# The first block of x loaded as two halves of 64 rows, one on each hardware DMA queue

## The chip, the cores and the metric

The kernel runs on one core of one Trainium2 chip. The metric is the device time of one execution in microseconds (us). The timed runs of the kernel before gave 225.97, 226.27 and 227.02 us, median 226.27.

## The reference

Two branches work on the same normalised x and are added to x: a local, dilated attention (A) and a gated mixer over the sequence (B). x is 2048 rows of 512, everything in bf16.

```python
x = A_x                                   # [1, 2048, 512]
xn = _layernorm(x, axis=-1)
return x + _A_ref(xn, A_wqkv, A_wo) + _B_ref(xn, B_w_in, B_w_sp, B_b_sp, B_w_out)

# A: 32 heads of 16; each position attends to 8 positions, 2 apart, up to itself
qkv = (xn @ wqkv) ...
logits = einsum('bhsd,bhswd->bhsw', q, kg) * scale ; softmax over the 8 ; times v ; @ wo

# B: w_in [512, 1792], w_sp [2048, 2048], w_out [896, 512]
z = _gelu(xn @ w_in)
z1 = z[..., :896] ; z2 = _layernorm(z[..., 896:])
g = einsum('ts,bsf->btf', w_sp, z2) + b_sp
return einsum('bsf,fd->bsd', z1 * g, w_out)
```

## The kernel before

The program is a list of tasks. Each task has an engine, what it reads and writes, and a name; a planner turns the reads and writes into semaphore waits. The order of the tasks on each engine is written out by hand in `plan.orders`: one list for TensorE (PE), ScalarE (ACT), VectorE (DVE), GpSimd (POOL) and the queue of SyncE (SP), in this order. Loads from HBM are issued by SP and by ACT, each into its own hardware queue. An engine takes its list strictly in order; a DMA stands in the list of the engine that issues it.

x is cut into 16 blocks of 128 rows. For each block b the planner has these tasks, all in `ln_block`: `bnst` (mean and variance statistics on DVE, L665), `bnag` (their aggregation on DVE, L668), `rstd` (the inverse root on POOL, L670), `norm` (subtract and multiply on DVE, L680). Blocks 0 to 3 are then transposed on PE (`xTr`, L696) and moved from PSUM to SBUF by ACT (`xTe`, L703); the others are transposed by DMA (`xTd`, L684).

Block 0 is treated apart, so that the first products can start before `rstd0` is there. Its rows are only centred: `ctr1` on DVE (columns 256 to 511, L673) and `ctr0` on ACT (columns 0 to 255, L675), transposed as `xTr0b` and `xTr0a`, and multiplied with w_in; `rstd0` comes in as a scale when the products are evacuated (`z2g`, L913). The products of blocks 0 to 3 with the second half of w_in are `z2_b_h` with a last letter a or b (L906): h is the half of the columns, b the half of the contraction that holds `w_in2a_1` or `w_in2b_1`, a the other. Block 0 uses half b first. The normalised block 0 for the attention is transposed later (`xNr`, L717).

The first loads are `ldx0` and `ldx1` on SP (L603), `ldw_in2a` and `ldw_in2b` in two halves each, half 0 on SP and half 1 on ACT (L608), `ldx2` on ACT, `ldx3` on SP. The next one on SP, `ldx4`, waits for `ldw_in2b_1`, and behind it stand `ldx5`, `ldx6` and `ldk` (the weights of K, L620). `ldk` and later `ldq` feed the products of Q and K (L749).

Before block 0 is there, PE runs `warm`: 29 matmuls of 146 columns on constants (L637). `fill0` (one of 256 columns) and `fill1` (three of 146) stand between the first transposes. On ACT the list begins with `actprime` (L643), which brings in the table for gelu.

The lists that matter at the start, in the kernel before:

```python
# PE
warm xTr0b fill0 xTr0a fill1 z2_0_0b z2_0_1b z2_0_0a xTr1a xTr1b z2_0_1a xNr z2_1_0a ...
# ACT
actprime ldw_in2a_1 ldw_in2b_1 ldx2 ctr0 xTe0b xTe0a xTe1a xTe1b xNe z2g0_0 ...
# DVE
zeros steps0 steps1 bnst0 bnag0 ctr1 bnst1 bnag1 norm0 norm1 bnst2 bnag2 bnst3 norm2 ...
# SP
ldx0 ldx1 ldw_in2a_0 ldw_in2b_0 ldx3 ldx4 ldx5 ldx6 ldk ldx7 ...
```

Of the kernel before, what the change touches and what calls it, by code (L numbers as in the profile page):

```python
# [328 lines left out]
def build_kernel(nc, A_x, A_wqkv, A_wo, B_x, B_w_in, B_w_sp, B_b_sp, B_w_out, out, report=False, sched_kw=None,  # L329
# [14 lines left out]
    x2 = A_x[0]  # L344
# [75 lines left out]
    with ExitStack() as es:  # L420
# [10 lines left out]
        def A(name, n, o2_=0):  # L431
            return ar[:, off[name] + o2_: off[name] + o2_ + n]

        def AC(o_, dims):
            return bass.AP(tensor=ar, offset=o_, ap=[[AR, 128]] + [list(d) for d in dims])

        def Fv(name, n, o2_=0):
            return fp[:, foff[name] + o2_: foff[name] + o2_ + n]
# [105 lines left out]
        def c_mm(n):  # L544
            return max(25.0, n / 2.4 + 2.6)

        def c_act(n, psum=True, accum=False):
            return 171.0 + n * 0.832 + (20.0 if accum else 0.0)
# [6 lines left out]
        def dma(eng, fn, nbytes, chan, reads=(), writes=(), name="", xbar=False, prio=None, lat=1700.0):  # L555
            return T(eng, fn, reads=tuple(reads), writes=tuple(writes), name=name, prio=prio,
                     dma=dict(chan=chan, nbytes=nbytes, xbar=xbar, lat=lat))
# [10 lines left out]
          name="steps0")  # L568
        T("dve", lambda v: v.memset(FCa(foff["st6"] + 8, [[9, NB], [1, 1]]), LN_EPS * D), writes=["st_eps"], est=160,
          name="steps1")  # L570
# [5 lines left out]
          writes=["ident"], est=350, name="ident1")  # L576
# [3 lines left out]
          writes=["nident"], est=350, name="nident1")  # L580
        T("pool", lambda g: g.memset(AC(off["KT"], [[KW, 4], [1, KP]]), 0.0),
          writes=[("KTpad", c, 0) for c in range(4)], est=200, name="ktpad", prio=2)
# [15 lines left out]
        def xin_ap(sl):  # L598
            return A("xin", 512, 512 * sl) if sl < 4 else A("xin2", 512, 512 * (sl - 4))

        def ld_x(b, eng="sp", after=()):
            sl = b % 8
            dma(eng, lambda e: e.dma_start(xin_ap(sl), x2[128 * b:128 * b + 128, :]), 128 * 512 * 2,  # L603
                ("xin", sl), reads=after, writes=[("xin", sl)], name="ldx%d" % b)
# [5 lines left out]
                    B_w_in[256 * h: 256 * h + 256, FH + lo: FH + lo + n].rearrange("(c p) n -> p c n", p=128)))(h),  # L610
                    256 * n * 2, (nm, h), writes=[(nm, h)], name="ld%s_%d" % (nm, h))

        ld_x(0)
        ld_x(1)
        ld_win_h("w_in2a", 0, HF)
        ld_win_h("w_in2b", HF, HF)
# [2 lines left out]
        for which, eng in ((0, "sp"), (1, "sp")):  # L619
# [4 lines left out]
                writes=[(("wq", "wk")[which], c) for c in range(4)],  # L624
                name="ld%s" % ("qk"[which]))
# [7 lines left out]
        def filler(n, name, est, prio=None, reads=(), w=512):  # L633
            def warm(t):
                last = None
                for i in range(n):
                    last = t.matmul(ps[:, 3584: 3584 + w], ones[:, :128], ones[:, :w], start=True, stop=True)  # L637
                return last
            T("pe", warm, reads=reads, writes=[("ps", 7)], est=est, name=name, prio=prio)
# [4 lines left out]
          est=-1200, name="actprime", tbl="gelu")  # L644
# [4 lines left out]
        def next_bank():  # L649
            k = ring[0]  # L650
            ring[0] = (k + 1) % NR[0]
            return k
# [8 lines left out]
        def ln_block(b):  # L661
            sl = b % 4
            xs_ = b % 8
            xin = xin_ap(xs_)
            T("dve", lambda v: v.bn_stats(Fv("st6", 6, 9 * b), xin),  # L665
              reads=[("xin", xs_)], writes=[("st6", b)],
              est=690, name="bnst%d" % b)
            T("dve", lambda v: v.bn_aggr(Fv("mv", 2, 2 * b), Fv("st6", 9, 9 * b)), reads=[("st6", b), "st_eps"],  # L668
              writes=[("mv", b)], est=180, name="bnag%d" % b)
            T("pool", lambda g: g.tensor_tensor(Fv("rstd", 1, b), Fv("mv", 1, 2 * b + 1), Fv("mhalf", 1), ALU.pow),  # L670
              reads=[("mv", b), "mhalf"], writes=[("rstd", b)], est=580, name="rstd%d" % b)
            if b == 0:
                T("dve", lambda v: v.tensor_scalar(A("attn", 256, 256), xin[:, 256: 512], Fv("mv", 1, 2 * b), None, ALU.subtract),  # L673
                  reads=[("xin", xs_), ("mv", b)], writes=[("xc", 1)], est=250, name="ctr1")
                T("act", lambda a: a.activation(A("attn", 256), xin[:, 0: 256], ACTF.Identity, bias=Fv("mv", 1, 2 * b),  # L675
                                                scale=-1.0),
                  reads=[("xin", xs_), ("mv", b)], writes=[("xc", 0)], est=400, name="ctr0")
            xo = off["attn"] + 1024 if b == 0 else off["xn"] + 512 * sl
            xk = "xn0" if b == 0 else ("xn", sl)
            T("dve", lambda v: v.tensor_scalar(AC(xo, [[1, 512]]), xin, Fv("mv", 1, 2 * b),  # L680
                                               Fv("rstd", 1, b), ALU.subtract, ALU.mult),
              reads=[("xin", xs_), ("mv", b), ("rstd", b)], writes=[xk], est=400, name="norm%d" % b)
            if b >= XDMA:
                dma("sp", lambda e: e.dma_start_transpose(AC(off["xnT"] + 128 * b, [[S, 4], [1, 128]]),  # L684
                                                          AC(xo, [[1, 512]])),
                    128 * 512 * 2, ("xT", sl), reads=[xk], writes=[("xnT", b)], name="xTd%d" % b, xbar=True)
            if b >= XDMA:
                return
            src, sk = (off["attn"], lambda h: ("xc", h)) if b == 0 else (xo, lambda h: xk)
            for h in ((1, 0) if b == 0 else (0, 1)):  # L690
                k = next_bank()

                def tr(t, h=h, k=k):
                    last = None
                    for i in range(2):
                        last = t.matmul(ps[:, 512 * k + 128 * i: 512 * k + 128 * i + 128],  # L696
                                        AC(src + 256 * h + 128 * i, [[1, 128]]), nident if b == 0 and h == 0 else ident,
                                        start=True, stop=True)
                    return last
                T("pe", tr, reads=[sk(h), "nident" if b == 0 and h == 0 else "ident"], writes=[("ps", k)], est=2 * c_mm(128), name="xTr%d%s" % (b, "ab"[h]))  # L700
                dst = (AC(off["attn"] + 512 + 256 * h, [[128, 2], [1, 128]]) if b == 0 else
                       AC(off["xnT"] + 2 * h * S + 128 * b, [[S, 2], [1, 128]]))
                T("act", (lambda dst, k: lambda a: a.activation(  # L703
                    dst, ps[:, 512 * k: 512 * k + 256].rearrange("p (c n) -> p c n", c=2), ACTF.Copy))(dst, k),
                  reads=[("ps", k)], writes=[("xcT", h) if b == 0 else ("xnTh", b, h)], est=c_act(256) - 30,
                  name="xTe%d%s" % (b, "ab"[h]))
            if b == 0:
                filler(cfg["fill0"], "fill0", 160.0 * cfg["fill0"], reads=[("xc", 1)], w=256)
                filler(cfg["fill1"], "fill1", 120.0 * cfg["fill1"], reads=[("xc", 0)], w=146)
# [389 lines left out]
        for j in range(NJ):  # L1099
# [8 lines left out]
            if j == 0:  # L1108
                for fn_, b, k0 in ((ln_block, 0, 3), (ln_block, 1, 1), (z2_block, 0, 5), (xn0_T, 0, 3), (ln_block, 2, 3), (z2_block, 1, 7),
                                   (z2_block, 2, 1), (ln_block, 3, 3), (z2_block, 3, 3)):  # L1110
                    ring[0] = k0
                    fn_(b)
                setup_masks()
                ring[0] = 5
            else:
                for b in bl:
                    ln_block(b)
            if j == 1:
# [5 lines left out]
                  name="biasf")  # L1124
# [146 lines left out]
        for t in range(NT):  # L1271
# [11 lines left out]
            if t >= 1:  # L1283
# [15 lines left out]
                out7_0 out5_0 P6_7 out4_0 P7_7 P3_7 P2_7 P4_7 out2_0 out3_0 out0_0 out1_1 out1_0 out1_2  # L1299
            """.split(),  # L1300
            """
                actprime ldw_in2a_1 ldw_in2b_1 ldx2 ctr0 xTe0b xTe0a xTe1a xTe1b xNe z2g0_0 xTe2a xTe2b z2g0_1 z2g1_0
                xTe3a xTe3b z2g2_0 z2g1_1 z2g3_0 z2g3_1 z2g2_1 QKe0_0 z2s0 QKe0_1 QKe0_2 QKe0_3 z2s1 QKe1_0 z2s2
                QKe1_1 halo0_2 QKe1_2 QKe1_3 z2s3 z2g4 halo0_1 z2g5 halo0_3 halo0_0 z2s4 halo1_1 halo1_0 z2g6 halo1_2
                z2g7 z2s5 QKe2_0 z2s6 QKe2_1 QKe2_2 z2s7 QKe2_3 z2g8 z2s8 z2g9 z2g10 z2s9 z2g11 z2s10 QKe3_0 z2s11
# [29 lines left out]
                rstd6 rstd7 rstd10 rstd8 rstd11 rstd9 rstd13 rstd14 rstd12 rstd15 hm2 zr0 zr1 zr2 zr3 srec1 srec0  # L1335
            """.split(),
            """
                ldx0 ldx1 ldw_in2a_0 ldw_in2b_0 ldx3 ldx4 ldx5 ldx6 ldk ldx7 ldx10 ldx8 ldq ldx11 xTd4 xTd5 xTd6 xTd7
                ldx9 ldx14 ldx13 ldx12 xTd10 xTd11 ldx15 xTd8 xTd9 ldwv xTd14 ldb xTd12 xTd13 xTd15 ldw_in1 w0_1 w0_0
                ldwout pT3 pT2 pT1 Vhalo0a Vzero w1_0 w1_1 ldwo1 ldwo2 ldwo3 ldwo0 Vhalo0b w2_0 w2_1 Vhalo1b Vhalo2b  # L1340
                pT0 uT15 uT14 OTd0 w3_0 w3_1 w4_0 uT12 w4_1 OTd1 uT13 Vhalo1a uT10 w5_0 OTd2 uT11 w5_1 uT8 uT9 w6_0
# [22 lines left out]
def bass_parallel_sum__sliding_local_dilated__mixer_gmlp__prompt_kernel(  # L1364
    nc, A_x, A_wqkv, A_wo, B_x, B_w_in, B_w_sp, B_b_sp, B_w_out, out
):
    build_kernel(nc, A_x, A_wqkv, A_wo, B_x, B_w_in, B_w_sp, B_b_sp, B_w_out, out)
# [28 lines left out]
```

## Time and profile before

| what | value |
|---|---|
| median of three timed runs | 226.27 us (225.97 to 227.02) |
| the profiled execution | 225.37 us, of which the span is 223.6 us |
| PE / DVE / ACT / POOL busy | 98% / 93% / 60% / 40% of the span |
| first warm-up matmul | 0.84 us |
| first transpose of block 0 | 4.41 us |
| first product with w_in | 5.22 us |
| DMA, from 0 to 5.22 us | 213 GB/s in the mean |

Times in the profile count from the start of the span. A row of the timeline gives start, length, engine, line, operation, output and input, the shapes, and how many instructions are merged in it; in brackets stands how long the engine was idle before, and what ended that. "PEld" is TensorE's loading of weights, which can run beside its matmuls. SPq and ACTq are the issues of DMAs by SP and ACT; their length is the issue alone, and the list of DMA issues tells how long after it the data had landed. Matmuls overlap in the records and their ends are modelled, so the distance from start to start is what one costs.

### The profile page before, as it was taken

Reading aid. Unit: us, or ns where it says so; the run is one execution under the profiler, and the core shown is the slowest. Engines: PE = TensorE matmul, PEld = TensorE weight load, DVE = VectorE, ACT = ScalarE, POOL = GpSimd, SP = SyncE. Lnnn points to the kernel's source line nnn. Section 1 sums busy time; section 2 is a strip of 40 time slices with the busy share of each in tenths; the row PEclk is TensorE's granted clock in tenths of the full one; section 3 lists DMA queues with packets and bytes.
Section 4 is the critical chain, followed back from the end, with each engine's and each line's share of the span. In section 5 each row is a group of like instructions: output and inputs, shape, how many; then the busy total and the mean of one; then the engine's idle time right before and its main releaser. Section 6 shows DMA issues by size and latency. Waiting matters only on the chain.

```text
span 223.6 us, 3124 instructions
## 1 busy us (share of the span) xinstructions
PE 219.7 (98%) x1166; PEld 122.4 (55%) x1180; DVE 207.3 (93%) x236; ACT 134.2 (60%) x241; POOL 89.6 (40%) x38
## 2 busy tenths in 40 slices
PE   8999999999999999999999999999999999999995
PEld 7555555554677776655555454544545544444544
DVE  4699999999999999999999999999999999999810
ACT  4769899999999999977333304324304216224442
POOL 4355559965000090000000899945999900000000
DMA  6884442790000002879689997949589696428352
GB/s 222 275 185 117 97 117 51 197 201 0 3 0 0 0 0 85 176 199 215 154 166 174 233 130 157 186 118 200 173 165 228 140 193 154 99 51 179 118 104 94
DMA packets 77716, 29.96 MB, mean 134 GB/s; under 512 B 68731, under 2 KB 75401, under 8 KB 77702
## 3 DMA queue, kind: packets, MB, share of 16 engines
q1 hardware_dynamic: 74566, 25.08, 53.2%
q10 hardware_dynamic: 3136, 4.69, 6.4%
q8 instruction: 9, 0.15, 0.3%
q14 instruction: 5, 0.04, 0.1%
HBM read 9.05 MB, written 2.10 MB: 50 GB/s over the span
## 4 chain that ended last, share of the span: by engine, by line
PE 98%; issue 0%; ACT 0%
PE ps L1044 38%; PE ps L749 12%; PE ps L926 11%; PE ps L1255 11%; PE ps L883 8%; PE ps L733 6%; PE ps L1251 6%; PE ps L906 3%; PE ps L637 2%; PE ps L807 1%; PE ps L696 0%; ACT arena L703 0%; ACT arena L1264 0%; PE ps L717 0%; PE ps L1237 0%
## 5 line engine op out<-in xcount | busy, mean ns | idle before, releaser
L1044 PE MATMUL ps<-arena 128*128 128x448 f16 (+1 forms) x448 | 86.7, 352 | 0.0
L866 POOL TENSOR_TENSOR arena<-arena,fpool 128x128 bf16<-128x128 f32 x2 | 49.9, 24946 | 45.6 <-DVE arena L862 45.6
L1044 PEld LDWEIGHTS ps<-arena 128*128 128x128 f16 (+1 forms) x448 | 43.8, 98 | 41.4
L1189 DVE TENSOR_TENSOR arena<-arena 128x4096 bf16<-128x4096 bf16 x16 | 36.2, 2282 | 0.0
L772 DVE TENSOR_TENSOR arena<-arena 128x8192 bf16<-128x8192 bf16 (+1 forms) x10 | 35.5, 3555 | 0.0
L955 POOL TENSOR_TENSOR fpool<-fpool 128x4 f32<-128x4 f32 x4 | 18.1, 4541 | 27.3 <-DVE fpool L952 27.3
L749 PE MATMUL ps<-arena 128*128 128x512 bf16 x124 | 27.7, 379 | 0.2
L1193 DVE TENSOR_TENSOR arena<-arena 128x4096 bf16<-128x4096 bf16 (+1 forms) x16 | 27.9, 1745 | 0.0
L1059 ACT ACTIVATE ps<-ps 128x448 f32<-128x448 f32 x16 | 8.4, 527 | 32.4 <-PE ps L1044 24.7
L1255 PE MATMUL ps<-arena 128*128 128x512 bf16 (+2 forms) x125 | 27.1, 355 | 0.1
L780 DVE TENSOR_TENSOR arena<-arena 128x4096 bf16<-128x4096 bf16 (+1 forms) x9 | 26.9, 2992 | 0.1
L926 PE MATMUL ps<-arena 128*128 128x448 bf16 x128 | 24.7, 352 | 0.0
L670 POOL TENSOR_TENSOR fpool<-fpool 128x1 f32<-128x1 f32 x16 | 17.4, 1088 | 16.0 <-DVE fpool L668 15.7
L1062 ACT ACTIVATE arena<-ps,fpool 128x448 bf16<-128x448 f32 x16 | 10.0, 635 | 22.3 <-PE ps L1044 22.3
L926 PEld LDWEIGHTS ps<-arena 128*128 128x128 bf16 x128 | 18.5, 144 | 5.9
L749 PEld LDWEIGHTS ps<-arena 128*128 128x128 bf16 x128 | 14.5, 113 | 13.0
L1264 ACT ACTIVATE arena<-ps 128x512 bf16<-128x512 f32 (+2 forms) x17 | 9.5, 563 | 16.8 <-PE ps L1255 16.8
L883 PE MATMUL ps<-arena 128*128 128x448 bf16 x96 | 19.1, 353 | 0.0
L1255 PEld LDWEIGHTS ps<-arena 128*128 128x128 bf16 x126 | 11.9, 98 | 12.4
L757 ACT ACTIVATE arena<-ps 128x1024 bf16<-128x1024 f32 x16 | 16.1, 1028 | 2.9 <-PE ps L749 2.8
L1251 PE MATMUL ps<-arena 128*128 128x512 bf16 (+2 forms) x65 | 15.3, 353 | 0.4
L938 ACT ACTIVATE arena<-arena 128x896 bf16<-128x896 bf16 x16 | 15.3, 956 | 0.0
(86 smaller groups left out, 256.1 us busy)
## 6 DMA issues: line engine op xcount, KB each, us to landing
arena<-in_A_x_dram ACTq DMA_DIRECT2D x8, 256.0 KB, 3.6
arena<-in_A_x_dram SPq DMA_DIRECT2D x15, 128.0 KB, 3.1
out_dram<-arena ACTq DMA_DIRECT2D x7, 256.0 KB, 2.3
arena<-in_A_wqkv_dram SPq DMA_DIRECT2D x3, 512.0 KB, 4.9
arena<-in_B_w_in_dram SPq DMA_DIRECT2D x1, 896.0 KB, 5.4
arena<-in_B_w_out_dram SPq DMA_DIRECT2D x1, 896.0 KB, 6.5
arena<-arena SPq DMA_DIRECT2D x2, 448.0 KB, 4.4
arena<-arena SPq DMA_DIRECT2D x1, 672.0 KB, 5.4
```

Of the source, the lines that this page charges most:

```text
L749: last = t.matmul(bank(k + which), AC(off["wqk"] + 1024 * dc + col0, [[4, 128]]), AC(off["xnT"] + dc * S + 512 * j, [[1, 512]]), start=(dc ...
L772: T("dve", lambda v: v.tensor_tensor(pbv, qb, kb, ALU.mult), reads=[(t_, c, j) for t_ in ("QT", "KT", "KTpad") for c in cs], writes=[("pb" ...
L780: T("dve", lambda v: v.tensor_tensor(av, av, bv, ALU.add), reads=[("pb", s_) for s_ in b], writes=[("pb", s_) for s_ in a], est=c_dve(4096 ...
L866: T("pool", lambda g: g.tensor_tensor(Rv, Zv, FCa(foff["mone"], [[0, 128]]), ALU.pow), reads=[kz, "mone"], writes=[kr], est=20000, name="s ...
L883: last = t.matmul(ps[:, 512 * (k + hf): 512 * (k + hf) + HF], AC(off["xnT"] + dc * S + 128 * b, [[1, 128]]), AC(off["w_in2"] + FH * dc + H ...
L926: lastm = t.matmul(ps[:, 512 * (k + hf): 512 * (k + hf) + HF], AC(off["xnT"] + dc * S + b, [[NTOK, 128]]), AC(off["w_in1"] + FH * dc + HF ...
L955: T("pool", lambda g: g.tensor_tensor(Fv("rstd2", 4, 4 * j), Fv("msq", 4, 4 * j), mhalf, ALU.pow), reads=[("msq", j), "mhalf"], writes=[(" ...
L1044: last = t_.matmul(pb_(k_), st(k), mv(k), start=(start and k == 0), stop=(k == 7), skip_group_check=True)
L1189: T("dve", (lambda iv, tv, av: lambda v: v.tensor_tensor(tv, iv, av, ALU.mult))(iv, tv, av), reads=[("attn", q // 4)] + [("V", i_) for i_ ...
L1193: T("dve", (lambda n: lambda v: v.tensor_tensor(AC(off["Vs"], [[4096, 2], [1, n]]), AC(off["Vs"], [[4096, 2], [1, n]]), AC(off["Vs"] + n, ...
L1251: t_.matmul(po, AC(off["OT"] + 1024 * (t % 3) + 512 * r_ + 128 * cc, [[1, 128]]), AC(off["wo"] + 512 * cc + c0, [[1, n]]), start=False, st ...
L1255: last = t_.matmul(po, AC(off["z1"] + FH * tb + 128 * fc, [[1, 128]]), AC(off["w_out"] + 512 * fc + c0, [[1, n]]), start=False, stop=(fc = ...
```

## The change

`ldx0` becomes `ldx0a` (rows 0 to 63, issued by SP, first in its list as `ldx0` was) and `ldx0b` (rows 64 to 127, issued by ACT, behind `actprime` and ahead of `ldw_in2a_1`). Each half has a semaphore of its own. `bnst0`, `ctr1`, `ctr0` and `norm0` are declared to read both halves; since `ctr1`, `ctr0` and `norm0` follow the statistics of block 0, only `bnst0` gets a wait for a second semaphore. The lists of PE, DVE and POOL stay as they are, and so does the count of warm-up matmuls; on DVE, `norm1` still stands ahead of `bnst2`.

```diff
-        ld_x(0)
+        for h in range(2):
+            dma(("sp", "act")[h], (lambda h: lambda e: e.dma_start(xin_ap(0)[64 * h: 64 * h + 64, :], x2[64 * h: 64 * h + 64, :]))(h),
+                64 * 512 * 2, (("xin", 0), "xin0b")[h], writes=[(("xin", 0), "xin0b")[h]], name="ldx0%s" % "ab"[h])
         ld_x(1)
...
             T("dve", lambda v: v.bn_stats(Fv("st6", 6, 9 * b), xin),
-              reads=[("xin", xs_)], writes=[("st6", b)],
+              reads=[("xin", xs_)] + (["xin0b"] if b == 0 else []), writes=[("st6", b)],
...
             if b == 0:
                 T("dve", lambda v: v.tensor_scalar(A("attn", 256, 256), xin[:, 256: 512], Fv("mv", 1, 2 * b), None, ALU.subtract),
-                  reads=[("xin", xs_), ("mv", b)], writes=[("xc", 1)], est=250, name="ctr1")
+                  reads=[("xin", xs_), "xin0b", ("mv", b)], writes=[("xc", 1)], est=250, name="ctr1")
                 T("act", lambda a: a.activation(A("attn", 256), xin[:, 0: 256], ACTF.Identity, bias=Fv("mv", 1, 2 * b),
                                                 scale=-1.0),
-                  reads=[("xin", xs_), ("mv", b)], writes=[("xc", 0)], est=400, name="ctr0")
+                  reads=[("xin", xs_), "xin0b", ("mv", b)], writes=[("xc", 0)], est=400, name="ctr0")
...
-              reads=[("xin", xs_), ("mv", b), ("rstd", b)], writes=[xk], est=400, name="norm%d" % b)
+              reads=[("xin", xs_), ("mv", b), ("rstd", b)] + (["xin0b"] if b == 0 else []), writes=[xk], est=400, name="norm%d" % b)
...
-                actprime ldw_in2a_1 ldw_in2b_1 ldx2 ctr0 xTe0b xTe0a xTe1a xTe1b xNe z2g0_0 xTe2a xTe2b z2g0_1 z2g1_0
+                actprime ldx0b ldw_in2a_1 ldw_in2b_1 ldx2 ctr0 xTe0b xTe0a xTe1a xTe1b xNe z2g0_0 xTe2a xTe2b z2g0_1 z2g1_0
...
-                ldx0 ldx1 ldw_in2a_0 ldw_in2b_0 ldx3 ldx4 ldx5 ldx6 ldk ldx7 ldx10 ldx8 ldq ldx11 xTd4 xTd5 xTd6 xTd7
+                ldx0a ldx1 ldw_in2a_0 ldw_in2b_0 ldx3 ldx4 ldx5 ldx6 ldk ldx7 ldx10 ldx8 ldq ldx11 xTd4 xTd5 xTd6 xTd7
```

## The prediction

> **What bounds the kernel now.** I read the page first: the busy time of each engine and the chain of work that ended last.
>
> ```profile
> span 223.6 us, 3124 instructions
> ...
> PE 219.7 (98%) x1166; PEld 122.4 (55%) x1180; DVE 207.3 (93%) x236; ACT 134.2 (60%) x241; POOL 89.6 (40%) x38
> ...
> PE 98%; issue 0%; ACT 0%
> ```
>
> TensorE (PE) is busy for 98% of the span, and the chain followed back from the last instruction is PE for 98% of it. So almost the whole kernel is one row of matmuls, and a change at the start counts by how far it moves the first useful matmul; behind that, PE has nothing to catch up with. Next I read the same chain in order of time at its beginning:
>
> ```profile
> 0.84 3.69 PE ps L637 x29
> 4.53 0.23 PE ps L696 x2
> ...
> 4.78 0.40 ACT arena L703
> ...
> 5.22 1.31 PE ps L906 x6
> ```
>
> The columns are start, length, what. L637 is the warm-up, 29 matmuls on constants; L696 the transposes of block 0 of x; L703 their evacuation by ScalarE (ACT); L906 the first products with w_in. The chain puts the warm-up ahead of the transposes, not the load of x. Ends of matmuls are modelled, so I looked at starts, in the timeline of PE alone and with its weight loads (PEld):
>
> ```profile
> 3.96 0.57 PE L637 MATMUL ps<-const-bfloat16-1.0 128*128 128x146 bf16 x3
> ...
> 4.08 0.45 PE L637 MATMUL ps<-const-bfloat16-1.0 128*128 128x146 bf16 x2
> ...
> 4.38 0.14 PEld L696 LDWEIGHTS ps<-arena 128*128 128x128 bf16 x2 [0.15 <-issue]
> 4.41 0.33 PE L696 MATMUL ps<-arena 128*128 128x128 bf16 x2
> 4.58 0.27 PE L637 MATMUL ps<-const-bfloat16-1.0 128*128 128x256 bf16 x1
> 4.69 0.28 PE L696 MATMUL ps<-arena 128*128 128x128 bf16 x2
> ```
>
> The last three warm-up matmuls start at 3.96, 4.08 and (the same step of 0.12 on) 4.20; the next slot is 4.32. The first transpose starts at 4.41. So PE stands idle for 0.09 us between the two, and its weight load (which takes the centred x) stood idle for 0.15. This 0.09 is all that an earlier x can win at this place, because PE takes its instructions in order and the 29 warm-up matmuls stay.
>
> What the transpose waits for is seen on VectorE (DVE):
>
> ```profile
> 3.02 0.69 DVE L665 BATCH_NORM_STATS2 fpool<-arena 128x6 f32<-128x512 bf16 x1 [1.61 <-DMA arena<-in_A_x_dram]
> 3.75 0.20 DVE L668 BATCH_NORM_AGGREGATE fpool<-fpool 128x2 f32<-128x9 f32 x1
> 3.98 0.29 DVE L673 TENSOR_SCALAR arena<-arena,fpool 128x256 bf16<-128x256 bf16 x1
> 4.18 0.69 DVE L665 BATCH_NORM_STATS2 fpool<-arena 128x6 f32<-128x512 bf16 x1
> ```
>
> bnst0 waits 1.61 us for x, then bnag0 and ctr1 follow with no gap to speak of; ctr1 ends at 3.98 + 0.29 = 4.27, and the weight load follows at 4.38. The two chains, warm-up and x, therefore meet within 0.09 us. A delay of x passes to PE in full; a gain is cut off at 0.09.
>
> **The change, part by part.** First the issues and their landings, from the timeline of the queues and from the list of DMA issues in narrow stretches (the last number is us from issue to landing, to one decimal):
>
> ```profile
> 0.80 0.40 SPq L603 DMA_DIRECT2D arena<-in_A_x_dram  x1
> 1.26 0.42 SPq L603 DMA_DIRECT2D arena<-in_A_x_dram  x1
> 1.72 0.95 SPq L608 DMA_DIRECT2D arena<-in_B_w_in_dram  x2
> 0.94 0.95 ACTq L608 DMA_DIRECT2D arena<-in_B_w_in_dram  x2
> 1.93 0.49 ACTq L603 DMA_DIRECT2D arena<-in_A_x_dram  x1
> 4.73 0.34 SPq L603 DMA_DIRECT2D arena<-in_A_x_dram  x1
> 6.06 0.44 SPq L620 DMA_DIRECT2D arena<-in_A_wqkv_dram  x1
> ```
>
> ```profile
> arena<-in_A_x_dram SPq DMA_DIRECT2D x1, 128.0 KB, 2.2
> arena<-in_A_x_dram SPq DMA_DIRECT2D x1, 128.0 KB, 2.8
> arena<-in_B_w_in_dram ACTq DMA_DIRECT2D x1, 224.0 KB, 2.8
> arena<-in_B_w_in_dram ACTq DMA_DIRECT2D x1, 224.0 KB, 3.3
> arena<-in_B_w_in_dram SPq DMA_DIRECT2D x1, 224.0 KB, 4.3
> arena<-in_A_x_dram ACTq DMA_DIRECT2D x1, 128.0 KB, 3.7
> arena<-in_A_wqkv_dram SPq DMA_DIRECT2D x1, 512.0 KB, 4.9
> ...
> arena<-in_B_b_sp_dram SPq DMA_DIRECT2D x1, 4.0 KB, 1.8
> ```
>
> In that order these are ldx0 (lands at 0.80 + 2.2 = 3.0), ldx1 (1.26 + 2.8 = 4.06), ldw_in2a_1 (0.94 + 2.8 = 3.74), ldw_in2b_1 (about 1.41 + 3.3 = 4.7), ldw_in2b_0 (about 2.19 + 4.3 = 6.5), ldx2 (1.93 + 3.7 = 5.63), ldk (6.06 + 4.9 = 10.96), and the smallest load of the kernel.
>
> *Block 0 in two halves.* SP still issues at 0.80, but 64 rows; ACT issues the other 64 rows at 0.94, where ldw_in2a_1 went out. bnst0 now needs both. No row shows a load of 64 rows, so I bound its landing. Early end: no faster than the 4 KB load, 1.8 us, which gives 0.94 + 1.8 = 2.74, that is 0.26 before 3.0. Late end: as slow as the first DMA of the ACT queue is now, with 3.5 times the bytes, 2.8 us: 0.94 + 2.8 = 3.74, 0.74 late. Between them stands the whole block's own 2.2: 0.94 + 2.2 = 3.14, 0.14 late. What speaks for the early side is the bandwidth, from the busy time by stretches (last two columns: DMA share and GB/s):
>
> ```profile
> 2.00:3.00 1.00, 1.00 (x11) 1.00 (x10) 0.00 (x0) 0.29 (x2) 0.25 (x2) 1.00 0.85 245
> 3.00:4.00 1.00, 1.00 (x11) 1.00 (x10) 0.91 (x3) 0.02 (x1) 0.00 (x0) 1.00 1.08 373
> ```
>
> From 2.00 to 3.00 the core moved 245 KB, nearly twice the 131 KB of block 0; the rest went to ldx1 and to ldw_in2a_1, which shared the engines with it. With both queues carrying x first, half of the traffic ahead of its landing goes away. I therefore take a landing about 0.1 us earlier than now, 2.9, nearest to the block's own row. Then ctr1 ends at 4.17, the weight load could stand at 4.28, and PE is free at 4.32: the transposes start at 4.32 and not at 4.41. Between 0 and 0.09, I count **0.05** us, since the weight load has itself to come ahead of the slot.
>
> The Trainium skill, DMA: Bandwidth & Descriptors, section Rules for kernel authors, says of two transfers to disjoint partition halves that they serialize, as both spread over the same 16 engines, and advises one transfer of 128 partitions. By that rule the split wins nothing, and the second half's landing goes with its issue, which is rival 1 below. No row of this trace shows a split load, so the trace neither agrees nor disagrees.
>
> *The second wait of bnst0.* Behind bnst0 on DVE stand bnag0, ctr1, bnst1 and all that follows, but they need block 0 anyway. DVE was idle for 1.61 us there, so a wait already fulfilled is hidden by that; uncovered it would cost about the gap between bnst0 and bnag0, 3.75 - 3.71 = 0.04. I count 0.
>
> *What ACT's queue moves.* One more issue of 0.40 to 0.49 us pushes ldw_in2a_1, ldw_in2b_1 and ldx2 back by about 0.45. ACT's own next work, ctr0, waits for DVE until 3.98, while the issues end at 1.93 + 0.49 + 0.45 = 2.87: covered. The data is wanted by these:
>
> ```profile
> 5.61 0.73 PE L906 MATMUL ps<-arena 128*128 128x448 bf16 x3
> 6.17 0.68 DVE L665 BATCH_NORM_STATS2 fpool<-arena 128x6 f32<-128x512 bf16 x1
> 6.31 0.27 PEld L696 LDWEIGHTS ps<-arena 128*128 128x128 bf16 x4 [0.22 <-DVE arena L680]
> 6.58 0.11 PEld L906 LDWEIGHTS ps<-arena 128*128 128x128 bf16 x2
> 12.15 3.75 PEld L749 LDWEIGHTS ps<-arena 128*128 128x128 bf16 x18
> ```
>
> ldw_in2a_1: 3.74 + 0.45 = 4.19 against the first product at 5.22, 1.0 us of cover. ldw_in2b_1: 4.7 + 0.45 = 5.15 against its first use, the third product at 5.61, 0.46 of cover. ldx2: 5.63 + 0.45 = 6.08 against bnst2 at 6.17, 0.09 of cover, and what stands behind bnst2 is the transpose of block 2, not the next matmul. Counted at 0; without their cover each costs PE what it is late. The SP queue's next issue behind ldx3 waits for ldw_in2b_1: ldx4 at 4.73 becomes about 5.18, and with it ldx5, ldx6 and ldk. ldk then lands at 10.96 + 0.45 = 11.41 against 12.15, when its weights are first loaded: 0.74 of cover.
>
> *What SP's queue moves.* ldx0a may be issued a little shorter (0.40 down to the 0.34 of the row at 4.73), so ldx1 and ldw_in2a_0 and ldw_in2b_0 go out 0 to 0.06 earlier, with fewer bytes of ACT's queue beside them. ldw_in2b_0 lands at 6.5 for a weight load at 6.58 that the transposes of block 1 precede; this is the tightest landing, and it gets looser. The transposes of block 1 load at 6.31 behind norm1; norm1's chain starts with bnst1 at 4.18, just behind ldx1's landing at 4.06, and moves with it. Counted at 0.
>
> *Sum.* 225.37 us for the profiled execution (its span of 223.6 and 1.77 around it) - 0.05 = 225.32. The profiled execution lies 0.90 under the median of the three timed runs, 226.27, so on that scale the forecast is 226.27 - 0.05 = 226.22, and the same 0.90 is added to each rival.
>
> **The rivals.**
>
> 1. *The second half comes later than the whole block did.* At 3.14 bnst0 is 0.14 late, ctr1 ends at 4.41, and PE waits: + 0.14, 226.4. At the far end, 3.74, it is + 0.74, 227.0. For it: the ACT queue issues 0.14 behind SP, and its first DMA took 2.8. Against it: that DMA had 224 KB.
>
> 2. *Slower by the clock.* The warm-up ran 146 columns in 0.12 us, 1.2 a ns; the 256-column filler at 4.58 was followed at 4.69, 2.3 a ns. So the array doubled its pace at about 4.5, though the granted clock reads 1.00 in both stretches above. If x is over 0.1 late, PE idles from 4.32 across this moment; if the doubling then fails and needs another stretch like the warm-up's 3.69 us at half pace, half of that is lost: + 1.85, 228.1. For it: the two moments lie within 0.2 us. Against it: 3.5 us of unbroken matmuls precede either way. The Trainium skill, TensorE: Matmul & The Clock Gate, Part 1, says that the clock is released after a busy window of about 3.4 us whose start does not depend on the kernel. The pace in these rows agrees with its two speeds; whether the window can be missed, no run here shows.
>
> 3. *The pushed-back weights arrive too late.* If ldw_in2b_1 needs the 4.3 us that the slowest load of its size took, it lands at 1.86 + 4.3 = 6.16, 0.55 behind its use: + 0.55, 226.8; the products behind it wait with it. Against it: DMA moves the same bytes in total.
>
> 4. *The gain is larger than the gap.* If the whole 0.26 of the early bound reached PE (were the warm-up not in the way): - 0.26, 226.0. Against it: the steps of 0.12 up to 4.20.
>
> **How the numbers follow.** Forecast 0.45; rival 1 0.23; rival 2 0.07; rival 3 0.12; rival 4 0.13. The predicted time is the forecast's, 226.2. The timed runs reach from 225.97 to 227.02, 1.05 wide, and the profiled execution was at 225.37, so a median of other runs can lie some tenths off by itself. The range goes from 225.3 (rival 4 less 0.7 of scatter) to 227.4 (the far end of rival 1 and 0.4 of scatter); it leaves rival 2 and the ends of scatter out, under 2 in 10. Half a per cent, 1.13 us, is about what a measurement of this kernel can tell from no change. Only rival 2 passes it by itself. To its 0.07 I add 0.08 for the far ends of rivals 1 and 3 with scatter on top: slower 0.15. No row carries a gain of 1.13; scatter on the forecast and on rival 4 gets 0.09. The rest, 0.76, is the same.
>
> **What would show it.** In the changed profile bnst0 should start between 2.76 and 3.0, the last warm-up matmul still near 4.20, the first transpose at 4.32 to 4.41, the first product at 5.13 to 5.22, and the products behind it in steps without new gaps. ACT should show three issues from 0.94 and ldx2 near 2.4; ldx4 about 0.45 later. A bnst0 after 3.1 with a transpose after 4.5 shows rival 1; products of 448 columns in steps of 0.37 after 5.2 rival 2; a gap before the third product rival 3. A span over 1 us away from 223.6 with the first product still near 5.2 would show that I looked at the wrong place.

## The result, and the profile after

| | kernel before | changed kernel |
|---|---|---|
| median of 22 runs each, taken side by side | 225.74 us (225.29 to 227.02) | 226.85 us (226.33 to 228.78) |
| ratio | | 1.0057, 95% interval 1.0040 to 1.0074 |
| profiled execution, its span | 225.37 us, 223.6 | 227.04 us, 225.3 |

The changed kernel is slower, by 1.11 us of the medians, which is 0.49%. The ratio, 1.0057, is that of the means; three runs of the changed kernel above 228.5 us pull it up. One lies just under and the other just over the half per cent, 1.13 us, that the prediction took as the bound of no change; the interval excludes a ratio of 1. The two profiled executions stand 1.67 apart, and the first thing to settle is which number is to be explained. The profiled execution of before was 0.37 under the median of these runs. A second profile of the kernel before, at 225.75 us and so at the median, is the better one to compare with; the profile of the changed kernel stands 1.29 above it. Its timeline of VectorE (DVE) and TensorE (PE):

```profile
3.44 0.69 DVE L665 BATCH_NORM_STATS2 fpool<-arena 128x6 f32<-128x512 bf16 x1 [2.03 <-DMA arena<-in_A_x_dram]
...
5.58 1.31 PE L906 MATMUL ps<-arena 128*128 128x448 bf16 x6
...
8.71 0.39 PE L696 MATMUL ps<-arena 128*128 128x128 bf16 x4
```

Here block 0 landed 0.4 us later than in the profile of the prediction, and the products with w_in started at 5.58 instead of 5.22; all six then ran through, the third at 5.58 + 2 x 0.19 = 5.96. The row at 8.71 is the transposes of block 2. Now the changed kernel. Its page, and the beginning of its chain in order of time (start, length, what):

```profile
span 225.3 us, 3126 instructions
...
PE 96%; DMA 2%; ACT 0%; issue 0%; ACTq 0%
```

```profile
0.80 0.68 ACT L645
...
1.52 0.78 ACTq L608
...
2.34 4.70 DMA arena<-in_B_w_in_dram
...
7.08 0.93 PE ps L908 x4
```

A load of w_in has entered the chain: 4.70 us of it, issued by ACT at 2.34, and PE goes on at 7.08. (The only load in the chain of the second profile of before is block 0 of x, 2.61 us.) The line numbers are two higher than before. The timeline of PE, its weight loads (PEld) and DVE shows the place:

```profile
3.35 0.69 DVE L667 BATCH_NORM_STATS2 fpool<-arena 128x6 f32<-128x512 bf16 x1 [1.95 <-DMA arena<-in_A_x_dram]
...
4.66 0.40 PE L698 MATMUL ps<-arena 128*128 128x128 bf16 x2
4.85 0.42 PE L639 MATMUL ps<-const-bfloat16-1.0 128*128 128x256 bf16 x1
5.06 0.42 PE L698 MATMUL ps<-arena 128*128 128x128 bf16 x2
...
5.85 0.76 PE L908 MATMUL ps<-arena 128*128 128x448 bf16 x2
7.08 0.93 PE L908 MATMUL ps<-arena 128*128 128x448 bf16 x4 [0.47 <-DMA arena<-in_B_w_in_dram]
...
7.91 0.70 DVE L667 BATCH_NORM_STATS2 fpool<-arena 128x6 f32<-128x512 bf16 x1 [1.32 <-DMA arena<-in_A_x_dram]
...
9.96 0.23 PEld L698 LDWEIGHTS ps<-arena 128*128 128x128 bf16 x4 [0.43 <-DVE arena L682]
9.97 0.40 PE L698 MATMUL ps<-arena 128*128 128x128 bf16 x4
```

PE runs the two products that need `ldw_in2a_1`, and then stands until `ldw_in2b_1` is there. The third product starts at 7.08, 1.12 us behind 5.96. `bnst2` too waits 1.32 us, for `ldx2`, and with it the transposes of block 2 come a little later still: 9.97 against 8.71, which is 1.26 of the 1.29 between the two executions. Block 0 itself was not the trouble: `bnst0` at 3.35 is no later than the 3.44 of before at its median.

One more thing in these rows could be taken for the cause. PE was at half pace from the transposes through the first two products: the filler of 256 columns at 4.85 is followed at 5.06, 0.21 later, where it was 0.11 in the rows of the prediction, and the two products take 0.76 us. By itself this would have held the third product until 5.85 + 0.76 = 6.61. It does not decide. In two other executions below, the second one of the changed kernel and the one with an unread load, the first two products ran at full pace (0.54 and 0.55 us), and the third still started only at 7.38 and 6.90.

The issues on both queues, and then the landings (last number, us from issue) of `ldw_in2a_1`, `ldw_in2b_1`, `ldw_in2b_0` and `ldx2`:

```profile
0.80 0.59 SPq L614 DMA_DIRECT2D arena<-in_A_x_dram  x1
1.45 0.56 SPq L603 DMA_DIRECT2D arena<-in_A_x_dram  x1
2.05 0.95 SPq L608 DMA_DIRECT2D arena<-in_B_w_in_dram  x2
...
0.94 0.55 ACTq L614 DMA_DIRECT2D arena<-in_A_x_dram  x1
1.52 0.79 ACTq L608 DMA_DIRECT2D arena<-in_B_w_in_dram  x1
2.34 0.49 ACTq L608 DMA_DIRECT2D arena<-in_B_w_in_dram  x1
```

```profile
arena<-in_B_w_in_dram ACTq DMA_DIRECT2D x1, 224.0 KB, 4.2
...
arena<-in_B_w_in_dram ACTq DMA_DIRECT2D x1, 224.0 KB, 4.7
...
arena<-in_B_w_in_dram SPq DMA_DIRECT2D x1, 224.0 KB, 5.0
arena<-in_A_x_dram ACTq DMA_DIRECT2D x1, 128.0 KB, 5.0
```

Two things went wrong at once. The issues became longer: a load of 64 rows takes 0.55 to 0.59 us to issue where the whole block took 0.40, and the load behind it takes 0.56 on SP and 0.79 on ACT. So `ldw_in2b_1` goes out at 2.34 and not at 1.41. And it takes 4.7 us instead of 3.3. It lands at 7.04, 2.3 us later than in the profile of the prediction and 2.0 later than in the second one of before (1.41 + 3.6 = 5.0).

### The profile page after: what moved, and what is told of

The parts are those of the page before. It is cut to its first block, busy times and chain, and to the rows that moved or that the text cites. A ratio compares the mean times of both kernels' runs of the same rounds, so it can differ in the third digit from the quotient of the medians.

```text
span 225.3 us, 3126 instructions
## 1 busy us (share of the span) xinstructions
PE 220.8 (98%) x1166; PEld 122.5 (54%) x1180; DVE 207.4 (92%) x236; ACT 134.3 (60%) x241; POOL 89.5 (40%) x38
## 4 chain that ended last, share of the span: by engine, by line
PE 96%; DMA 2%; ACT 0%; issue 0%; ACTq 0%
PE ps L1046 38%; PE ps L751 12%; PE ps L928 11%; PE ps L1257 11%; PE ps L885 8%; PE ps L735 6%; PE ps L1253 6%; PE ps L908 3%; DMA arena<-in_B_w_in_dram 2%; PE ps L809 1%; PE ps L698 0%; ACTq L608 0%; ACT L645 0%; ACT arena L1266 0%; PE ps L719 0%
```

## The experiments

The theories: (1) the weights of ACT's queue are late, because a load was put ahead of them and because of the order in which two queues are served; (2) the halves of 64 rows are slow in themselves; (3) the first packets of w_in are slow, which shows only when x no longer runs beside them. All ratios are to the kernel before on the same chip.

**An extra load of 64 rows on ACT, block 0 whole.** The load goes to a place that is read only much later, after it is written anew.

```diff
         ld_x(0)
+        dma("act", lambda e: e.dma_start(A("Za", 512)[64: 128, :], x2[64: 128, :]), 64 * 512 * 2, "spare", writes=["Za"], name="ldspare")
...
-                actprime ldw_in2a_1 ldw_in2b_1 ldx2 ctr0
+                actprime ldspare ldw_in2a_1 ldw_in2b_1 ldx2 ctr0
```

> Block 0 is loaded whole by SP as in the kernel before; ACT first issues a load of 64 rows of x into a place nobody reads until much later, then its weights. Theory 1, starved weights (what hurts is a small issue ahead of the weights on ACT's queue): bnst0 starts at 3.0 to 3.1 as before, but ldw_in2b_1 is issued over 0.5 us later than its 1.41 and lands near 7.0, PE waits for it, and the time is 0.8 to 1.3 us over the kernel before. Theory 2, slow halves (what hurts is that block 0 itself lands 0.33 us later, and with it the start of PE at half clock): bnst0 at 3.0, first product at 5.2, time within 0.3 us of before.

227.0 us, 1.0063 (1.0040 to 1.0087): as slow as the changed kernel. In its timeline:

```profile
3.17 0.69 DVE L666 BATCH_NORM_STATS2 fpool<-arena 128x6 f32<-128x512 bf16 x1 [1.76 <-DMA arena<-in_A_x_dram]
...
5.88 0.55 PE L907 MATMUL ps<-arena 128*128 128x448 bf16 x2 [0.63 <-DMA arena<-in_B_w_in_dram]
6.90 0.93 PE L907 MATMUL ps<-arena 128*128 128x448 bf16 x4 [0.47 <-DMA arena<-in_B_w_in_dram]
```

Block 0 is on time and the third product is at 6.90, in an execution 0.34 under its median. The loss needs no split of block 0; a small load ahead of ACT's weights is enough.

**Both halves on SP.**

```diff
-            dma(("sp", "act")[h], ...
+            dma("sp", ...
...
-                actprime ldx0b ldw_in2a_1 ...
+                actprime ldw_in2a_1 ...
...
-                ldx0a ldx1 ldw_in2a_0 ...
+                ldx0a ldx0b ldx1 ldw_in2a_0 ...
```

> Both halves of block 0 are issued by SP, one behind the other; ACT's list is that of the kernel before. Theory 1: ldw_in2b_1 is issued near 1.4 and lands near 4.7 again; SP's own weights go out one issue later, so ldw_in2b_0 lands 0.4 to 0.5 us later than 6.5 and PE waits at most that: 0.3 to 0.6 us over before. Theory 2: the two loads of 64 rows take 0.55 to 0.6 us each to issue as in the changed kernel, bnst0 starts after 3.4, and the time is at least as bad as the changed kernel's, 1.1 us or more over before.

227.44 us, 1.0071 (1.0047 to 1.0094). ACT's weights go out early again, from 0.94, but now block 0 and block 1 are late:

```profile
0.94 1.22 ACTq L608 DMA_DIRECT2D arena<-in_B_w_in_dram  x2
...
4.42 0.69 DVE L667 BATCH_NORM_STATS2 fpool<-arena 128x6 f32<-128x512 bf16 x1 [3.02 <-DMA arena<-in_A_x_dram]
...
8.58 0.40 PE L698 MATMUL ps<-arena 128*128 128x128 bf16 x4 [0.79 <-DVE arena L682]
```

The time is what theory 2 expected, but its cause is mixed: SP's two issues took 1.22 us together, and `ldx1` behind them landed at 6.45. It doesn't tell the theories apart. It does show that a long issue reaches over to the other queue: ACT's list holds no load of 64 rows here, and its two weights took 1.22 us to issue where 0.95 was usual, `ldx2` 0.62 where it was 0.49.

**The changed kernel with the two halves of ACT's weights as one load.**

```diff
+            if nm == "w_in2a":
+                dma("act", lambda e: e.dma_start(
+                    AC(off["w_in2"] + 2 * FH, [[FH, 2], [1, FH]]),
+                    B_w_in[256: 512, FH: 2 * FH].rearrange("(c p) n -> p c n", p=128)),
+                    256 * FH * 2, (nm, 1), writes=[("w_in2a", 1), ("w_in2b", 1)], name="ldw_in2_1")
-            for h in range(2):
+            for h in range(1):
...
-                actprime ldx0b ldw_in2a_1 ldw_in2b_1 ldx2 ctr0
+                actprime ldx0b ldw_in2_1 ldx2 ctr0
```

> The changed kernel, but ldw_in2a_1 and ldw_in2b_1 are one DMA of 448 KB, so ACT issues three loads ahead of its work, as many as the kernel before. Theory 1: the bytes are queued one issue earlier, the weights land by 5.6, PE's wait for them goes, and the time is within 0.4 us of before. Theory 2: bnst0 still starts near 3.35 and the time stays 0.8 to 1.3 us over before.

227.4 us, 1.0071 (1.0046 to 1.0096), spread from 226.46 to 229.05. One issue fewer doesn't cure it: the load goes out at 1.52, takes 0.79 to issue and lands at 6.4 (in an execution 0.67 under the median). Theory 1 was too simple where it counted issues only.

**Halves of 256 columns instead of 64 rows.** The same bytes on the same queues, but each half has all 128 rows.

```diff
-xin_ap(0)[64 * h: 64 * h + 64, :], x2[64 * h: 64 * h + 64, :]
+xin_ap(0)[:, 256 * h: 256 * h + 256], x2[0: 128, 256 * h: 256 * h + 256]
```

> The changed kernel, but the halves are 256 columns of all 128 rows each, not 64 rows of all columns. Theory 1: as the changed kernel, ldw_in2b_1 near 7.0 and 0.8 to 1.3 us over before. Theory 2, if it is the 64 rows that make the issue slow: issues of 0.40 to 0.43 us, first bytes near 1.7 us, and the time within 0.4 us of before.

226.3 us, 1.0022 (1.0010 to 1.0034): about half of the loss is gone, which is between what the two theories expected.

```profile
0.80 0.40 SPq L614 DMA_DIRECT2D arena<-in_A_x_dram  x1
...
0.94 0.39 ACTq L614 DMA_DIRECT2D arena<-in_A_x_dram  x1
1.36 0.97 ACTq L608 DMA_DIRECT2D arena<-in_B_w_in_dram  x2
...
2.92 0.69 DVE L667 BATCH_NORM_STATS2 fpool<-arena 128x6 f32<-128x512 bf16 x1 [1.51 <-DMA arena<-in_A_x_dram]
...
6.89 0.93 PE L908 MATMUL ps<-arena 128*128 128x448 bf16 x4 [0.63 <-DMA arena<-in_B_w_in_dram]
```

Issues are back at 0.39 and 0.40, the loads behind them at their usual length, and `bnst0` starts at 2.92. So the long issue belongs to the 64 rows and not to the 64 KB. What is left, 0.5 us, goes with the load ahead of the weights: PE still waits for `ldw_in2b_1`, until 6.89 in this execution, which was 0.4 over its median.

**Halves of columns and one load for ACT's weights.** Both edits above together.

> Block 0 in two halves of columns, one on each queue, and ldw_in2a_1 and ldw_in2b_1 as one load of 448 KB. Theory 1: the bytes ahead of the last byte of these weights are 720 KB again as in the kernel before, they land between 5.5 and 6.1, all six first products start behind that without a gap, and the time is 0.2 to 0.5 us over before. Theory 3: the hole in the rate stays, the weights land after 6.2, 0.6 us or more over before.

225.96 us, 1.0004 (0.9994 to 1.0014): the loss is gone.

```profile
5.85 1.31 PE L913 MATMUL ps<-arena 128*128 128x448 bf16 x6 [0.77 <-DMA arena<-in_B_w_in_dram]
```

```profile
arena<-in_B_w_in_dram ACTq DMA_DIRECT2D x1, 448.0 KB, 4.4
```

Issued at 1.35, it lands at 5.75, and all six products run through. This agrees with theory 1 as it stood by then, bytes ahead and time of issue, and is better than the 0.2 to 0.5 us it was given. It gains nothing over before, so no version tried here beats the kernel before.

**`ldx2` ahead of ACT's weights, nothing split.**

```diff
-                actprime ldw_in2a_1 ldw_in2b_1 ldx2 ctr0
+                actprime ldx2 ldw_in2a_1 ldw_in2b_1 ctr0
```

> The kernel before with ldx2 moved to the head of ACT's loads: three loads on ACT as before, 128 rows, no byte more, block 0 whole. Theory 1, turns (the two queues take turns load by load, so what counts is how many bytes stand ahead of ldw_in2b_1): the turns become x0, x2, x1, w_in2a_1, w_in2a_0, w_in2b_1, some 360 KB more ahead of its last byte, it lands at 6.2 to 6.9, the third product starts there instead of 5.61, and the time is 0.5 to 1.1 us over before. Theory 2, it is the load of 64 rows that hurts: ACT's issues stay near 0.45 us and the time is within 0.3 us of before.

227.01 us, 1.0042 (1.0027 to 1.0058). ACT's issues are short (0.38, then 0.97 for two), no byte is added, and still:

```profile
6.62 0.93 PE L906 MATMUL ps<-arena 128*128 128x448 bf16 x4 [0.47 <-DMA arena<-in_B_w_in_dram]
```

Order alone costs nearly as much as the change: 1.03 us of the medians, in seven runs. This execution was 0.42 under their median.

**The kernel before with ACT's weights as one load.** The edit to the weights is that of the two experiments with one load above; block 0 is loaded whole by SP.

> The kernel before with ldw_in2a_1 and ldw_in2b_1 as one load of 448 KB on ACT, so one issue fewer stands there and ldx2 goes out 0.45 us earlier. By the theory of turns both halves land together near 4.7, ahead of the first product at 5.22, and the time is the same as before or up to 0.3 us below it; if the first product then waits for all 448 KB beyond 5.3, it is 0.1 to 0.5 us above.

226.36 us, 1.0020 (1.0009 to 1.0031), above what was expected for a landing near 4.7 (it landed at 4.8). PE had no wait for the weights, but block 1 was late: `ldx1`, issued at 1.26, took 4.0 us. The rows of the two queues (q10 is ACT's, q1 is SP's: packets, MB, share of the 16 engines) show what moved meanwhile. The first is this kernel from 3.50 to 3.75; no row of q1 stands beside it:

```profile
q10 hardware_dynamic: 57, 0.10, 105.5%
```

The next pair is the first profile of the kernel before, from 2.75 to 3.00:

```profile
q10 hardware_dynamic: 95, 0.08, 97.8%
q1 hardware_dynamic: 1, 0.00, 1.2%
```

In these stretches the load of one queue had nearly all the engines while a load of the other queue, issued 0.3 us behind it, waited. In the kernel before this worked out well: x0, w_in2a_1, x1, w_in2b_1 landed in the order in which they are wanted. With a load put ahead on ACT, `ldw_in2a_0` of SP gets ahead of `ldw_in2b_1`, which is wanted first. By issue and time to landing, `ldw_in2a_0` came at 5.3 against 4.7 in the kernel before, at 6.45 against 7.04 in the changed one, at 6.3 against 6.5 with `ldx2` ahead, and at 5.7 against 6.8 with halves of columns. With ACT's weights as one load besides, it came behind them again, at 6.4 against 5.75, and there the loss was gone. With halves of rows and one load it came behind them as well, at 6.7 against 6.4, and they were late all the same, so this order is not all of it.

**A touch of w_in first.** The unread load of the first experiment takes its 64 rows from w_in.

```diff
-x2[64: 128, :]), 64 * 512 * 2, "spare"
+B_w_in[256: 320, FH: FH + 512]), 64 * 512 * 2, "spare"
```

> As the kernel with the unread load of 64 rows on ACT, but these rows are of w_in and not of x. Theory 3, first touch (the hole in the DMA rate between 3.0 and 4.0 us is there because the first packets of w_in are slow when nothing else runs beside them): the hole of 60 to 160 GB/s goes, the third product starts by 6.4, the time is at most 0.8 us over before. Theory 1: the source of the small load makes no difference, the hole stays, third product near 6.9, 1.0 to 1.4 us over before.

227.58 us, 1.0076 (1.0049 to 1.0103). The rate of the DMA engines (last number, GB/s) still has its hole:

```profile
3.25:3.50 0.25, 1.00 0.38 62
3.50:3.75 0.25, 1.00 0.59 168
```

The third product started at 7.13, in an execution at 228.57 us whose granted clock fell to 0.50 from about 7.2 on. Theory 3, in this form, fails. What makes the hole, which the changed kernel has too (150, 68 and 215 GB/s in the quarters from 3.25 to 4.00, where the kernel before moved 365 to 386), stays open.

**Halves of 256 columns, the second one on GpSimd's queue.**

```diff
-            dma(("sp", "act")[h], ... xin_ap(0)[64 * h: 64 * h + 64, :], x2[64 * h: 64 * h + 64, :]
+            dma(("sp", "pool")[h], ... xin_ap(0)[:, 256 * h: 256 * h + 256], x2[0: 128, 256 * h: 256 * h + 256]
...
-                actprime ldx0b ldw_in2a_1 ...
+                actprime ldw_in2a_1 ...
...
-                mhalf ident0 ...
+                ldx0b mhalf ident0 ...
```

> Halves of columns, the second one issued by GpSimd on its own queue, ahead of its constants; the lists of ACT and SP stand as before. Theory 1: ldw_in2a_1 and ldw_in2b_1 are issued at 0.94 and 1.41 and land before 5.2 and 5.6, PE has no gap behind the first product, and the time moves only by how late the second half lands: within 0.3 us of before if bnst0 starts by 3.1. If a split of block 0 in itself costs, by its second wait or by the engines it shares, the time is 0.5 us or more over before with bnst0 by 3.1.

228.39 us, 1.0102 (1.0078 to 1.0126), and no answer: the edit moved more than it meant to.

```profile
1.29 0.72 POOL L614 DMA_DIRECT2D arena<-in_A_x_dram  x1 [0.78 <-POOLq L1383]
...
2.17 1.07 ACTq L608 DMA_DIRECT2D arena<-in_B_w_in_dram  x2
...
6.30 2.59 PE L908 MATMUL ps<-arena 128*128 128x448 bf16 x6
```

GpSimd issued at 1.29 only, its constants came behind that, `actprime` on ACT waits for one of them, and ACT's weights stand behind `actprime`: out at 2.17 instead of 0.94. The first six products took 2.59 us, where 1.31 was usual.

**Block 0 late, the weights untouched.** SP issues `ldx1` ahead of `ldx0`.

```diff
-                ldx0 ldx1 ldw_in2a_0 ...
+                ldx1 ldx0 ldw_in2a_0 ...
```

> The kernel before with ldx1 issued ahead of ldx0 by SP; ACT's loads are untouched, so block 0 alone is late. If a late block 0 costs PE in full, as the prediction has it: ldx0 issued at 1.26, bnst0 at 3.4 to 3.7, transposes 0.3 to 0.6 us after 4.41, and the time 0.3 to 0.6 us over before, with no gap behind the first product. If the weights alone decide: within 0.2 us of before.

226.63 us, 1.0052 (1.0028 to 1.0075): 0.83 over before, more than expected. Eight of its twelve runs lie between 226.37 and 227.09, four between 228.16 and 228.54. The profile fell among the four:

```profile
4.19 0.69 DVE L665 BATCH_NORM_STATS2 fpool<-arena 128x6 f32<-128x512 bf16 x1 [2.78 <-DMA arena<-in_A_x_dram]
...
6.54 2.44 PE L906 MATMUL ps<-arena 128*128 128x448 bf16 x6
```

`bnst0` starts at 4.19, later than the 3.4 to 3.7 expected, and PE stands for 1.05 us ahead of the first transpose, at 5.58 against 4.83 in the second profile of before. So a late block 0 does cost PE, as the prediction said; the eight shorter runs, whose median is 0.67 over before, fit that, but none of them has a profile. On top of it this execution took 2.44 us for six products instead of 1.31: PE at half pace, until after 9.5 (from the start of one product, at 9.21, to the next, at 9.58, is still 0.37), while the granted clock in the trace reads 1.00 throughout. Whether the late block brought that on is not shown.

**The two kernels once more.**

> The changed kernel once more, for a second profile. If the lateness of ldw_in2b_1 belongs to the order of the loads, it lands after 6.3 again and PE has a gap ahead of the third product; if it was an accident of one execution, it lands before 5.6 and the first products run through.

> The kernel before once more, for a second profile. The loads on ACT issued at 0.94 and 1.41 again, ldw_in2b_1 landed by 5.2, no gap among the first products over 0.2 us.

The second profile of before stands at the head of this part. The second one of the changed kernel was at 228.71 us. The order of loads did the same again: issues of 0.59, 0.56, 0.54 and 0.79, `ldw_in2b_1` out at 2.34 and landed at 7.3. On top of it came the clock. First PE's rows:

```profile
6.24 0.54 PE L908 MATMUL ps<-arena 128*128 128x448 bf16 x2 [0.79 <-DMA arena<-in_B_w_in_dram]
7.38 1.68 PE L908 MATMUL ps<-arena 128*128 128x448 bf16 x4 [0.61 <-DMA arena<-in_B_w_in_dram]
```

Here PE waited for `ldw_in2a_1` too, which landed at 1.52 + 4.6 = 6.1. The busy time by stretches (PE's is the first number behind the length; the granted clock is third from the end):

```profile
6.50:7.00 0.50, 0.27 (x2) 0.00 (x0) 0.10 (x1) 0.00 (x0) 0.00 (x0) 1.00 1.02 352
7.00:7.50 0.50, 0.12 (x1) 0.12 (x2) 0.00 (x0) 0.00 (x0) 0.00 (x0) 0.63 0.56 194
7.50:8.00 0.50, 0.50 (x2) 0.16 (x2) 0.18 (x1) 0.00 (x0) 0.00 (x0) 0.50 0.09 31
...
10.00:11.00 1.00, 1.00 (x8) 0.77 (x7) 0.42 (x2) 0.31 (x1) 0.68 (x3) 0.73 0.65 180
```

PE's two waits for weights, 0.79 and 0.61 us long, were followed by a granted clock of 0.50 from about 7.2 to 10.5. The execution lost 1.86 us to the median of the changed kernel. Of its 22 timed runs three are like that (228.54, 228.59 and 228.78, with a mean granted clock of 0.992); none of the 22 runs of before is above 227.02.

## Why the prediction failed

**Right.** PE sets the end, and a shift of its first products passes to the end: + 1.12 us at the third product and + 1.26 at the transposes of block 2, for + 1.29 between the two executions. With halves of columns, which is not the change that was forecast, the load of block 0 and the transposes came about as forecast: `bnst0` at 2.92 in one profile and 3.07 in the other, the first transpose at 4.32 and 4.37.

**Right by number only.** The price of the clock in rival 2, + 1.85, was met by the three runs that had it, + 1.7 to + 1.9, but by another mechanism. Rival 2 had the doubling of the pace fail at about 4.5. In the second profile of the changed kernel, whose mean granted clock of 0.992 is that of the three, it had not failed; the clock fell back at about 7.2, behind the waits for the weights. A doubling that came only after 9.5 was seen with `ldx1` ahead. And what strikes three runs of 22 does not make the median.

**The step that failed.** "ldw_in2b_1: 4.7 + 0.45 = 5.15 against its first use, the third product at 5.61, 0.46 of cover", "Counted at 0". It landed at 7.04. Two terms in it were wrong. The delay of the issue was taken as one issue of the usual length, 0.45; it was 0.93, since a load of 64 rows takes longer to issue and slows the one behind it. And the time from issue to landing was carried over as 3.3; it was 4.7, since that number did not hold for the new order of loads on the two queues. Rival 3 named this place and had + 0.55. It was the right mechanism, with half the price and a chance of 0.12.

**The gain itself.** The - 0.05 of the sum rested on a landing at 2.9. The second half landed at 0.94 + 2.3 = 3.24, `bnst0` started at 3.35 and the first transpose at 4.66, which is the prediction's own sign of rival 1. But that rival's price is not what was paid: the transposes are no later than the 4.83 of before at its median, and the third product waited for its weights anyway.

**Of the same kind.** `ldw_in2a_1` was to land at 4.19, with 1.0 us of cover; it landed at 5.7, and in the second profile PE stood 0.79 for it. `ldx2` was to land at 6.08 and did at 2.86 + 5.0 = 7.86; its part is the 0.14 by which 1.26 exceeds 1.12. "ldw_in2b_0 ... gets looser" was wrong: SP's loads went out later too (`ldx1` at 1.45 instead of 1.26), and it landed at 7.5 instead of 6.5. `ldx4`, which waits for `ldw_in2b_1`, was forecast for 5.18 and went out at 7.05; no wait of PE for `ldk` behind it is seen, as its cover moved along with PE.

**The gap of 0.09 us** on which the gain was built belonged to one execution. In the second profile of before, block 0 lands 0.4 us later, and PE idles for about 0.5 us between the warm-up and the transposes. More could have been won there than was counted; the changed kernel's `bnst0`, 3.35 and 3.37 against 3.02 and 3.44, shows that it did not win it. The Trainium skill's rule, DMA: Bandwidth & Descriptors, section Rules for kernel authors, that two halves of the partitions are not worth splitting, stood against the change, and these profiles agree as far as they go: the second half of the rows landed at 3.24, the whole block at 3.0 and 3.4. The prediction gave it as a rival of + 0.14 us, and counted at 0 what the second load does to those behind it.

**Not settled:** why 64 rows take longer to issue than 128 of half the length, and what the hole in the DMA rate is. How the loss divides, about half to the rows and half to the load ahead of the weights, is read from the medians with columns and with rows, + 0.52 and + 1.11, and is rough: `ldx2` ahead, 128 KB with no load of 64 rows, cost + 1.03. When PE's pace doubles is open too: in these profiles it was anywhere from before 4.3 (the touch of w_in) to after 9.5 (`ldx1` ahead).

## What to carry to other kernels

A load's time to landing is a property of the whole order of loads, not of the load. If one is put ahead on a queue, work out anew which bytes go first on both queues, and hold every landing behind it against its first use. Where a stage turns on tenths of a microsecond at the start, take a second profile before calling a gap of 0.09 a bound.

## What was not expected of the hardware

- A load of 64 rows of 1 KB took 0.54 to 0.59 us to issue on either queue; 128 rows of 512 B, the same bytes, took 0.38 to 0.40. 128 rows of 1 KB took 0.38 to 0.40 too, so the length of a row is not it. The load issued behind 64 rows took 0.56 to 0.79, where 0.42 to 0.45 was usual.
- Waits of PE of 0.79 and 0.61 us, close together in the first 7.4 us, were followed by a granted clock of 0.50 for about 3 us, and so were waits of 0.98 and 0.56 in the profile with the touch of w_in; waits of 0.63 and 0.47 in that of the unread load of x were not. That the waits are the cause is likely and was not tested. The Trainium skill, TensorE: Matmul & The Clock Gate, section HAM oscillation — how this bites in real kernels, warns of idle gaps over 3.4 us; these were shorter, and here the measurement decides.
- The granted clock read 1.00 in stretches in which PE ran at half pace, in the first profile of the changed kernel up to the third product and with `ldx1` ahead until after 9.5. There the distance from start to start told the pace, and the clock did not.
